# Fused attention and feed-forward on one core: the first pair's tokens kept in transposed order, an addition in unlike shapes, one query tile in another buffer, and a planner with new numbers

## The chip, the core and the metric

One core of a Trainium2 chip runs the whole program. The metric is the device time of one launch in microseconds. A core has a tensor engine (PE, for matmuls, with weight loads shown as PEld), VectorE (DVE), ScalarE (ACT), GpSimd (POOL) and SyncE (SP, whose queue issues every DMA of this kernel), all with instruction streams of their own that meet by semaphores.

## What is computed

Eight batches of eight heads with 576 tokens of 64 values each. A short set of 32 queries per head attends to the tokens, and then the tokens attend to those 32 results. The output of all heads, 512 values for each of 4608 tokens, goes through a feed-forward with GELU.

```python
def sm_attn(qq, kk, vv):
    s = scale * np.matmul(qq, kk.transpose(0, 1, 3, 2))
    s = s - np.max(s, axis=-1, keepdims=True)
    a = np.exp(s)
    a = a / (np.sum(a, axis=-1, keepdims=True) + 1e-09)
    return np.matmul(a, vv)
p_packed = sm_attn(p, k, v)
out = sm_attn(q, p_packed, p_packed)      # [8, 8, 576, 64]
x = out.transpose(0, 2, 1, 3).reshape(4608, 512)
h = x @ w_in                              # [512, 2048]
g = 0.5 * h * (1.0 + erf(h * inv_sqrt2))
return g @ w_out                          # [2048, 512]
```

## The kernel before

**Stages.** The batches are worked on in four pairs. For a pair, the attention gives two things: the packed result `pp` (32 values per head) and the weights `a2` of the second softmax. The product a2 x packed is never made: `packed_w_in` forms W' = packed x W_in for each batch, and the hidden layer is W' x a2. W_in and W_out are taken in four pieces of 512 hidden columns, so there are 16 units u = 4 x pair + piece. A unit has eight steps, four blocks c of 128 hidden columns for each batch j of the pair. In step n PE makes h (`hidden_steps`, L1117 for unit 0 and L1126 for the others), ACT applies GELU (`graw`, L1148) and rounds it to the high half of g (L1155), DVE makes the low half (L1157), and PE adds g x W_out into four PSUM tiles with three matmuls each (`three`, L1178 to L1180, twelve o matmuls per step). The 64 tokens per batch that fill no tile of 128 are cast on POOL (L1168, L1169) and multiplied as the edge tile (`o_edge`). `finish` copies or adds the sums to `acc` (L1259, L1264) and the last unit of a pair stores them (L1269). Unit 0 uses plain float32 for h, in 8 matmuls per step instead of 12 of the rounded type.

**Loads.** Keys and queries come as two tiles of 576 KB per batch (`load`), for the first pair as whole rows (L499), for later pairs as four DMAs with short rows (L509). The weights come as 64-bit words of 512 KB (L984, L988). In the first four units they are decoded by ACT (L994, L995), DVE (L1002 to L1008) and POOL (L1022 to L1036), stored as float32 (`keep`, L1041), and read back by later pairs (L962).

**The first pair's attention.** Keys and queries are transposed by PE (L537) and copied back (L541), the packed queries at L574. The first scores are at L602, the softmax at L669 to L695, the packed result at L744 to L762. The second scores come back transposed by DVE (L780). Then each group of 32 weights gets its maximum (L798) taken off (L823), the exponential (L829), its sum (L837), EPS added (L838), the reciprocal (L839) and the product (L842), the last transpose into `a2` (L848, in the first pair, where it also restores the order of tokens with a strided write; L854 in the others) and the split into two rounded halves (L856, L858). One of the four chunks of the first pair has L823 and L842 on POOL.

**What sets the order.** `Order` runs the whole program as a set of tasks in a model with a cost in us for each operation, once dry and once for good, and writes out the instructions of each engine in the order in which the model issued them. Priorities come from the chain of operations behind each one, with the tables `SLACK` and `EARLY` by kind of task. `LATER` and `FIRST` hold the steps of attention stages and of loads. A `Ring` is a set of buffers with a fixed order of users. In the result each engine, SP's queue too, executes strictly in its order and waits at the first instruction that isn't ready. Where the model has PE with nothing to do before the first output step, it writes a filler, a small matmul on zeros (`keep_warm`, L1099). In steady state an operation on PE that isn't of a step is taken as ready `MARGIN` = 2 us later than the model says.

Of the kernel before, what the change touches and what calls it, by code (L numbers as in the profile page):

```python
# [42 lines left out]
DMA_FIRST, DMA_ISSUE, DMA_START, DMA_END, DMA_RATE = 2.0, 0.5, 0.6, 0.9, 390e3  # L43

DMA_DEPTH = 8
TABLE_SWITCH = 1.3
PE_START, PE_WINDOW, PE_LEAST = 1.0, 3.41, {True: 0.45, False: 0.9}
# [4 lines left out]
    "batch0": 1.967,  # L52
    "batch1": 2.254,
    "attention": 2.432,
    "load0": 0.822,
    "load": 4.206,
    "w_in0": 3.279,
    "w_out0": 2.28,
    "w_in": 1.0,
    "w_out": 1.839,  # L60
    "packed_w_in": 1.201,
# [3 lines left out]
    "batch0": 0,  # L65
    "batch1": 2.3,
    "attention": 0,
    "load0": 0.7,
    "load": -23.7,
    "w_in0": -0.9,  # L70
    "w_out0": -0.6,
    "w_in": 0,
    "w_out": -10.3,
    "packed_w_in": -2.4,
    "steps": -3.6,
}

MARGIN = 2.0

# [14 lines left out]
    "weights2": (31.8, 53.8, 41.5, 53.2),  # L94
    "groups1": ((0, 1, 2, 3),),
# [23 lines left out]
    "copy": ("ACT", "ACT", "ACT", "ACT"),  # L119
    "banks": (True, False, False, True),  # L120
# [5 lines left out]
    "turn": {"k": ("DVE", "ACT", "ACT", "ACT"), "q": ("ACT", "DVE", "ACT", "ACT")},  # L126
# [80 lines left out]
def tails_of(done):  # L207

    tails, of = {}, [0.0] * len(done)
    for n in reversed(range(len(done))):  # L210
        key, time, by, kind = done[n]
        of[n] += time * SLACK[kind]
        tails[key] = of[n] + EARLY[kind]
        for x in by:
            of[x] = max(of[x], of[n])
    return tails
# [10 lines left out]
class Order:  # L227
# [4 lines left out]
    def __init__(self, tails=None):  # L232
# [7 lines left out]
        self.free[PE] = PE_START  # L240

# [24 lines left out]
    def advance(self, task, value, engine):  # L266
# [16 lines left out]
        if isinstance(what, Op):  # L283
# [11 lines left out]
            entry = (0 if self.dry else -self.tails[key], self.serial, what, lambda v, e: go_on(v, e, by), after)  # L295
# [34 lines left out]
    def issue(self, engine):  # L330
# [15 lines left out]
        if engine == DMA:  # L346
            n, size = op.cost
            end = self.now
            for _ in range(n):
                end = max(end, self.under_way[-DMA_DEPTH])  # L350
                self.link = max(self.link, end + DMA_ISSUE + DMA_START) + size / n / DMA_RATE
                end += DMA_ISSUE
                self.under_way.append(max(self.link, end + DMA_START) + DMA_END)
# [33 lines left out]
def packed_attention_gelu_ffn(ctx: ExitStack, tc: tile.TileContext, q, k, v, p, w_in, w_out, out):  # L387
# [27 lines left out]
    def plan(order):  # L415
# [6 lines left out]
        def small(b):  # L422

            return psum_o if b < 2 else wide
# [14 lines left out]
        mx2s = ring("mx2", 2, [P, 3, 4, NB32])  # L439
# [14 lines left out]

        wps[1].names = ["v_0_1"] + [f"wp_{u}_1" for u in range(NU)]
# [32 lines left out]
        class Chunk:  # L488
            def __init__(self, bt, hh):
                self.bt, self.b, self.hh, self.i, self.n = bt, bt.b, hh, 2 * bt.j + hh, f"{bt.b}_{hh}"  # L490
# [4 lines left out]

        def load(bt, name, src, c, step):

            def rows(t):
                nc.sync.dma_start(t, src[bt.b, 4 * c:4 * c + 4].rearrange("h (x s) d -> (h x) (s d)", s=2 * NT))  # L499
# [11 lines left out]
            cost, fn = ((1, 590e3), rows) if bt.b < 2 else ((4, 1475e3), blocks)  # L511
            bt.raw[name, c] = yield Op(DMA, cost, step, fn, [(xraws, f"{name}_{bt.n}_{c}")])
            fire(bt.loaded[name, c])

        def transposed(bt, name, c, step):
            yield bt.loaded[name, c]
            raw = bt.raw[name, c]
            if bt.b < 2:
# [3 lines left out]
                yield [turn(raw, t, i, engine, step, f"{name}m_{bt.n}_{c}_{i}", hold) for i in range(3)]  # L522
# [6 lines left out]
            xraws.give(raw)  # L529
# [22 lines left out]
        def load_values(s, step):  # L552
# [8 lines left out]
            s.v = yield Op(DMA, (2, 660e3), step, fn, [(s.v_ring, f"v_{s.n}")])  # L561
            fire(s.v_loaded)

        def packed_queries(bt, step):
# [11 lines left out]
            m = yield Op(PE, 0.22, step, product, [(small(bt.b), f"pTm_{bt.n}")])  # L576
# [5 lines left out]
            small(bt.b).give(m)  # L582
# [116 lines left out]
        def packed(s, step):  # L699

            e1T = yield Op(PE, 0, step, lambda t: None, [(e1ts, f"e1T_{s.n}")], busy=False, hold=held("packed", s))
            ring_ = small(s.b)
# [92 lines left out]
        def greatest2(s, step):  # L795
            yield Op(
                DVE, 0.67, step,
                lambda: nc.vector.tensor_reduce(s.mx2[:, 0, s.i], blocks(s.e2), axis=AX.X, op=ALU.max))  # L798
# [17 lines left out]
        def softmax2(ss, step):  # L816
            n, m = len(ss), ss[0].mx2

            def centre(s):
# [3 lines left out]
                    lambda: on(engine).tensor_tensor(u, u, per_block(m[:, 0, s.i]), ALU.subtract), port=True)  # L823
# [519 lines left out]
```

## Time and profile before

| | |
|---|---|
| median of 3 runs | 744.21 us (743.89 to 745.51) |
| span of the profiled execution, first to last instruction | 740.1 us |
| its own time | not on the page; the median lies 4.1 us above its span |
| PE busy | 726.6 us, 98% |
| DVE, ACT, POOL busy | 391.8, 350.8, 149.3 us |
| granted clock of PE | 0.999 |
| moved by DMA | 106.75 MB, 83.89 read from and 22.02 written to HBM |

A row of a group of instructions reads: line, engine, operation, out<-in by the program's names, shapes, count, then busy time and mean duration of one in ns, and after the second bar the idle time of the engine just before them, with what ended it. A row of a timeline reads: start, duration, engine, line, and in brackets the idle time ahead of it and who ended it. A row of a window reads: from:to, its length, then busy time (and instructions) of PE, PEld, DVE, ACT and POOL, the granted clock, the mean DMA share and GB/s. `SPq` is the issue of a DMA by SP, not its transfer. Records of PE overlap: an o matmul's record lasts 0.39 us, and the next one starts 0.23 us after it.

### The profile page before, as it was taken

Reading aid. Unit: us, or ns where it says so; the run is one execution under the profiler, and the core shown is the slowest. Engines: PE = TensorE matmul, PEld = TensorE weight load, DVE = VectorE, ACT = ScalarE, POOL = GpSimd, SP = SyncE. Lnnn points to the kernel's source line nnn. Section 1 sums busy time; section 2 is a strip of 40 time slices with the busy share of each in tenths; the row PEclk is TensorE's granted clock in tenths of the full one; section 3 lists DMA queues with packets and bytes.
Section 4 is the critical chain, followed back from the end, with each engine's and each line's share of the span. In section 5 each row is a group of like instructions: output and inputs, shape, how many; then the busy total and the mean of one; then the engine's idle time right before and its main releaser. Section 6 shows DMA issues by size and latency. Waiting matters only on the chain.

```text
span 740.1 us, 13183 instructions
## 1 busy us (share of the span) xinstructions
PE 726.6 (98%) x5292; PEld 583.6 (79%) x5292; DVE 391.8 (53%) x614; ACT 350.8 (47%) x597; POOL 149.3 (20%) x312
## 2 busy tenths in 40 slices
PE   8999999998999999999999999999999999999997
PEld 5778776886778788788777878788877888888886
DVE  4798748887775323723767331652558322333332
ACT  5866667765653343733455343463455344323321
POOL 1446453644310001010010101010011011101010
PEclk9999999999999999999999999999999999999999
DMA  9999984685417994252143996332141602112031
GB/s 298 356 152 305 208 245 165 206 236 195 171 59 211 182 171 153 33 171 65 46 184 95 206 174 233 40 118 88 33 171 58 243 1 99 74 47 96 1 114 71
DMA packets 156157, 106.75 MB, mean 144 GB/s; under 512 B 123841, under 2 KB 132033, under 8 KB 156097
## 3 DMA queue, kind: packets, MB, share of 16 engines
q1 hardware_dynamic: 156096, 105.93, 53.7%
q8 instruction: 41, 0.67, 0.4%
q14 instruction: 20, 0.16, 0.1%
HBM read 83.89 MB, written 22.02 MB: 143 GB/s over the span
## 4 chain that ended last, share of the span: by engine, by line
PE 78%; DMA 10%; DVE 4%; ACT 3%; SPq 2%; issue 2%; POOL 1%; DVEq 0%; ACTq 0%; POOLq 0%
PE h L1126 23%; PE o L1178 14%; PE o L1180 13%; PE o L1179 13%; DMA k<-in_k_dram 4%; PE wps L1060 3%; DMA wraw<-in_moe_w_out_dram 3%; PE s L602 2%; PE o_edge L1178 2%; DMA wraw<-in_moe_w_in_dram 2%; PE o_edge L1180 2%; PE o_edge L1179 2%; PE pp L744 1%; SPq L509 1%; DMA q<-in_q_dram 1%
## 5 line engine op out<-in xcount | busy, mean ns | idle before, releaser
L1126 PEld LDWEIGHTS h<-a2T,wp 128*128 128x128 f32 x1440 | 202.2, 188 | 17.1 <-ACT graw L1148 2.2
L1126 PE MATMUL h<-a2T,wp 128*128 128x288 f32 x1440 | 211.3, 296 | 2.4 <-ACT graw L1148 0.8
L1178 PE MATMUL o<-w,g 128*128 128x512 f32 x508 | 205.4, 404 | 0.3 <-ACT g L1155 0.3
L1180 PE MATMUL o<-w,g 128*128 128x512 f32 x508 | 199.5, 393 | 1.7 <-DVE g L1157 1.7
L1179 PE MATMUL o<-w,g 128*128 128x512 f32 x508 | 198.4, 391 | 0.0
L1148 ACT ACTIVATE graw<-h 128x576 f32<-128x576 f32 x128 | 83.3, 651 | 241.6 <-PE h L1126 223.2
L1157 DVE TENSOR_TENSOR g<-graw,g 128x512 fp32r<-128x512 f32 x128 | 92.8, 725 | 169.5 <-ACT g L1155 168.9
L1168 POOL CAST t<-graw 128x64 fp32r<-128x64 f32 x128 | 37.1, 290 | 492.3 <-ACT graw L1148 360.6
L1178 PEld LDWEIGHTS o<-w,g 128*128 128x128 f32 x508 | 95.5, 188 | 41.3 <-issue 21.3
L1180 PEld LDWEIGHTS o<-w,g 128*128 128x128 f32 x508 | 95.4, 188 | 26.4 <-DVE g L1157 5.2
L1179 PEld LDWEIGHTS o<-w,g 128*128 128x128 f32 x508 | 95.5, 188 | 14.4
L1264 DVE TENSOR_TENSOR acc<-o,acc 128x512 f32<-128x512 f32 x96 | 63.7, 684 | 40.5 <-PE o L1180 40.5
L1155 ACT CAST g<-graw 128x512 fp32r<-128x512 f32 x128 | 79.4, 621 | 9.3 <-PE o L1180 6.0
L1076 DVE TENSOR_TENSOR wp<-wps,wp 128x1024 fp32r<-128x1024 f32 x30 | 36.7, 1222 | 36.2 <-ACT wp L1071 36.2
L1071 ACT CAST wp<-wps 128x1024 fp32r<-128x1024 f32 x30 | 30.4, 1012 | 44.0 <-PE wps L1060 44.0
L1169 POOL TENSOR_TENSOR t<-graw,t 128x64 fp32r<-128x64 f32 x128 | 46.6, 364 | 10.2
L1060 PE MATMUL wps<-w,pp 64*32 64x512 f32 (+1 forms) x528 | 34.6, 581 | 0.6 <-DVE e L780 0.6
L994 ACT ACTIVATE wt<-wraw 128x512 f32<-128x512 f32 x32 | 21.6, 675 | 23.9 <-DMA wraw<-in_moe_w_out_dram 9.6
L526 DVE STREAM_TRANSPOSE kT<-k 128x1152 f32<-128x1152 f32 x12 | 16.5, 1376 | 26.9 <-DMA k<-in_k_dram 26.9
L1030 POOL TENSOR_TENSOR wt<-wt 128x512 int32<-128x512 int32 x16 | 20.7, 1296 | 39.4 <-DVE wt L1008 30.2
L1022 POOL TENSOR_TENSOR w<-wt 128x512 int32<-128x512 int32 x16 | 21.7, 1357 | 29.5 <-ACT kT L541 12.5
L1002 DVE TENSOR_SCALAR wt<-wt 128x512 f32<-128x512 f32 x32 | 16.5, 516 | 19.5 <-ACT wt L994 19.4
(115 smaller groups left out, 673.6 us busy)
## 6 DMA issues: line engine op xcount, KB each, us to landing
w<-ws SPq DMA_DIRECT2D x72, 512.0 KB, 4.9
ws<-w SPq DMA_DIRECT2D x24, 512.0 KB, 4.2
out_dram<-acc SPq DMA_DIRECT2D x36, 256.0 KB, 2.7
wraw<-in_moe_w_in_dram SPq DMA_DIRECT2D x16, 512.0 KB, 5.5
v<-in_v_dram SPq DMA_DIRECT2D x16, 512.0 KB, 6.1
wraw<-in_moe_w_out_dram SPq DMA_DIRECT2D x16, 512.0 KB, 4.8
k<-in_k_dram SPq DMA_DIRECT2D x48, 144.0 KB, 4.7
q<-in_q_dram SPq DMA_DIRECT2D x48, 144.0 KB, 4.6
```

The costliest lines, as they stand in the source:

```text
L1060: nc.tensor.matmul(t[r0:r0 + 32, hh, :m], lhsT=pp[b][rows, hh, r0:r0 + 32], rhs=wi[u, hh][rows, g, cols], start=True, stop=True)
L1076: yield Op(DVE, 1.2, step, lambda: nc.vector.tensor_tensor(lo, x, hi.bitcast(F32), ALU.subtract))
L1126: nc.tensor.matmul(t[:, half, :HALF], lhsT=w[:, wpart, ch, fc], rhs=a2T[b, ch][:, apart, half * HALF:(half + 1) * HALF], start=ch == 0 and ...
L1148: lambda raw: nc.scalar.activation(raw.rearrange("p (a n) -> p a n", a=2), t[:, :, :HALF], AF.Gelu),
L1155: g = yield Op(ACT, 0.52, lead, lambda g: nc.scalar.copy(g[:, 0], main), [(gts, f"g_{n}")])
L1157: DVE, 0.6, lead, lambda: nc.vector.tensor_tensor(g[:, 1], main, g[:, 0].bitcast(F32), ALU.subtract),
L1168: nc.gpsimd.tensor_copy(dst[:, 0], side)
L1169: nc.gpsimd.tensor_tensor(dst[:, 1], side, dst[:, 0].bitcast(F32), ALU.subtract)
L1178: nc.tensor.matmul(t, lhsT=g[0], rhs=w[:, 0], start=first, stop=False)
L1179: nc.tensor.matmul(t, lhsT=g[0], rhs=w[:, 1], start=False, stop=False)
L1180: nc.tensor.matmul(t, lhsT=g[1], rhs=w[:, 0], start=False, stop=last)
L1264: yield Op(DVE, 0.6, n, lambda: nc.vector.tensor_tensor(a, x, a, ALU.add))
```

## The change

**The first pair's tokens.** The last transpose of `weights2` writes contiguously and leaves the tokens in the order (n, x) instead of x * 18 + n. All that follows works on tokens alike, so the order stays until `finish` stores the rows of pair 0 with a strided view of the output. The middle tile holds tokens of both batches and takes two DMAs instead of one.

**EPS.** The buffer of the second softmax's sums gets three columns more, the sums are laid out as 3 groups of 6 with a pitch of 7, and the addition reads that and writes 18 in a row.

**A query tile.** `q_0_1`, the second query tile of batch 0, goes into the buffer that later holds the first W', as `v_0_1` did with the second.

**PSUM.** All second scores of the first pair take a wide tile (`banks` all False). 

**The planner.** DMA operations have new costs, and a short-row load counts as two of the DMAs under way. In steady state an operation that waits for a DMA is taken as ready `DMA_MARGIN` = 3 us later. A change between PE instructions on the whole array and in parts costs 0.1 us in the model. A later pair's attention starts when the given output step (`from`: the third, or the first) has its g. Single tasks get offsets of priority (`SOONER`), and `SLACK` and `EARLY` have new numbers.

```diff
-DMA_FIRST, DMA_ISSUE, DMA_START, DMA_END, DMA_RATE = 2.0, 0.5, 0.6, 0.9, 390e3
+DMA_FIRST, DMA_ISSUE, DMA_START, DMA_END, DMA_RATE = 2.5, 0.5, 0.6, 0.9, 390e3
+MODE_SWITCH = 0.1
 SLACK = {
-    "load": 4.206,
+    "load": 0.122,
...
 EARLY = {
-    "load": -23.7,
+    "load": 21.2,
...
+SOONER = {
+    "softmax2_0_1": -53.3,
...
+DMA_MARGIN = 3.0
...
+    "from": (2, 0, 2, 0),
...
-    "banks": (True, False, False, True),
+    "banks": (False, False, False, False),
+    "small": (True, True, True, True),
+    "together": True,
...
+            if engine == DMA and self.steady:
+                after += DMA_MARGIN
+            first = 0 if self.dry else -self.tails[key] - SOONER.get(key, 0) - (SOONER.get(what.takes[0][1], 0) if what.takes else 0)
...
+            if engine == PE and op.cost and op.busy != self.whole:
+                self.whole = op.busy
+                begin += MODE_SWITCH
...
-        mx2s = ring("mx2", 2, [P, 3, 4, NB32])
+        mx2s = ring("mx2", 2, [P, 3, 4, NB32 + 3])
...
+        wps[0].names = ["q_0_1"] + [f"wp_{u}_0" for u in range(NU)]
...
+        def raw_ring(bt, name, c):
+            return wps[0] if (bt.b, name, c) == (0, "q", 1) else xraws
...
-            cost, fn = ((1, 590e3), rows) if bt.b < 2 else ((4, 1475e3), blocks)
+            cost, fn = ((1, 590e3), rows) if bt.b < 2 else ((4, 1640e3, 2), blocks)
...
-            s.v = yield Op(DMA, (2, 660e3), step, fn, [(s.v_ring, f"v_{s.n}")])
+            s.v = yield Op(DMA, (2, 830e3), step, fn, [(s.v_ring, f"v_{s.n}")])
...
             def inverse():
-                nc.vector.tensor_reduce(z, u, axis=AX.X, op=ALU.add)
-                nc.vector.tensor_scalar(z, z, EPS, None, ALU.add)
-                nc.vector.reciprocal(r, z)
+                apart = z.rearrange("p (a b) -> p a b", a=3)[:, :, :NB32 // 3]
+                nc.vector.tensor_reduce(apart, u.rearrange("p (a b) n -> p a b n", a=3), axis=AX.X, op=ALU.add)
+                nc.vector.tensor_scalar(r, apart, EPS, None, ALU.add)
+                nc.vector.reciprocal(r, r)
...
-                yield Op(
-                    DVE, 1.3, step,
-                    lambda: nc.vector.transpose(raw.rearrange("p (x n) -> p n x", n=NB32), blocks(s.e2)))
+                yield Op(DVE, 0.69, step, lambda: nc.vector.transpose(raw, s.e2))
...
-                if n % STEPS == 0:
+                yield g_ready[n]
+                if n % STEPS == LATER["from"][n // STEPS]:
                     fire(pair_started[n // STEPS])
-                yield g_ready[n]
...
-                yield Op(DMA, (1, 262e3), n, lambda: nc.sync.dma_start(out[r0:r0 + P], a))
+                def fn():
+                    if pr:
+                        nc.sync.dma_start(out[r0:r0 + P], a)
+                        return
+                    for j in range(2):
+                        rows = out[j * S:(j + 1) * S].rearrange("(x n) d -> n x d", n=NB32)
+                        n0, n1 = max(4 * i - j * NB32, 0), min(4 * i + 4 - j * NB32, NB32)
+                        if n0 < n1:
+                            p0 = 32 * (n0 + j * NB32 - 4 * i)
+                            nc.sync.dma_start(rows[n0:n1], a[p0:p0 + 32 * (n1 - n0)])
+                yield Op(DMA, (1 if pr or i != 4 else 2, 262e3), n, fn)
```

More of the change, by code (lines that the diff above doesn't have):

```diff
@@ L521, in transposed @@
                 hold = FIRST["hold"][name][2 * bt.j + c]
-                yield [turn(raw, t, i, engine, step, f"{name}m_{bt.n}_{c}_{i}", hold) for i in range(3)]
+                yield [turn(raw_of(raw), t, i, engine, step, f"{name}m_{bt.n}_{c}_{i}", hold) for i in range(3)]
             else:
@@ L581, in packed_queries @@
                 [(pts, f"pT_{bt.n}")])
-            small(bt.b).give(m)
+            small(2 * bt.j, bt.b).give(m)
             fire(bt.p_ready)
@@ L873, in attention @@
             for bt in bts:
-                kind = "attention" if pr else f"batch{bt.j}"
-                loading = "load" if pr else "load0"
-                start(packed_queries(bt, plan["p"][bt.j]), kind)
+                start(packed_queries(bt, plan["p"][bt.j]), "attention" if pr else f"batch{bt.j}")
                 for c in range(2):
-                    start(load(bt, "k", k, c, plan["k"][2 * bt.j + c]), loading)
-                    start(load(bt, "q", q, c, plan["q"][2 * bt.j + c]), loading)
+                    for name, src in (("k", k), ("q", q)):
+                        start(load(bt, name, src, c, plan[name][2 * bt.j + c]), "load" if pr else "load0")
             for s in ss:
@@ L882, in attention, with kind_of @@
                 s.v_ring = wps[1] if (s.b, s.hh) == (0, 1) else vraws
-                start(load_values(s, plan["v"][s.i]), loading)
+                start(load_values(s, plan["v"][s.i]), "load" if pr else "load0")
+            def kind_of(s, which):
+                return f"attention {which}" if pr else f"batch{s.j} {which}_{s.n}"
             def group(members, softmax, step):
@@ L891, in task @@
                     fire(after)
-                start(task(), "attention" if pr else f"batch{members[0] // 2}")
+                start(task(), kind_of(ss[members[0]], softmax.__name__))
                 return {i: (before, after) for i in members}
@@ L965, in weight @@
                 return
-            yield [decode(u, i, part, *at) for part, at in enumerate(zip(load_steps, steps))]
+            kind = f"w_{'in' if i < 2 else 'out'}"
+            yield [
+                (decode(u, i, part, *at), kind if u else f"{kind}0 {n}_{part}")
+                for part, at in enumerate(zip(load_steps, steps))]
             d = scratch[f, i] = None if order.dry else dram.tile([P, 2, FB], F32, name=f"ws_{f}_{i}")
@@ L1280, in later_pair @@
             yield scored[pr - 1]
-            plan = {key: x if "groups" in key else [(pr - 1) * STEPS + y for y in x] for key, x in LATER.items()}
+            plan = {key: x if key in ("from", "groups1", "groups2") else [(pr - 1) * STEPS + y for y in x] for key, x in LATER.items()}
             yield from attention(pr, plan)
```

105 lines of the change are left out of this document (69 added, 36 removed).

## The prediction

> **What bounds the kernel now.** I read the page first, then busy time by stretches, then the tensor engine's timeline for each stretch in which it loses time, and last the queue behind that loss.
>
> ```profile
> span 740.1 us, 13183 instructions
> PE 726.6 (98%) x5292; PEld 583.6 (79%) x5292; DVE 391.8 (53%) x614; ACT 350.8 (47%) x597; POOL 149.3 (20%) x312
> 0.00:57.00 57.00, 53.76 (x664) 39.62 (x665) 41.43 (x84) 40.00 (x81) 20.01 (x25) 1.00 1.00 267
> 100.00:120.00 20.00, 18.69 (x148) 13.86 (x147) 14.12 (x24) 13.51 (x26) 12.24 (x17) 1.00 0.72 254
> 170.00:176.00 6.00, 4.35 (x21) 3.23 (x20) 4.07 (x5) 3.80 (x8) 2.10 (x2) 1.00 0.43 171
> 244.00:258.00 14.00, 13.01 (x79) 9.55 (x78) 6.87 (x7) 5.60 (x9) 1.11 (x4) 1.00 1.18 197
> 418.00:433.00 15.00, 14.26 (x86) 10.69 (x85) 7.08 (x7) 5.84 (x10) 1.41 (x5) 1.00 1.30 196
> 57.00:736.00 679.00, 672.56 (x4631) 544.00 (x4628) 349.67 (x530) 310.85 (x517) 129.26 (x288) 1.00 0.51 134
> L1099 PE MATMUL idle<-still 128*128 128x256 bf16 x180 | 25.2, 285 | 1.1 <-DVE still L411 1.1
> L1126 PE MATMUL h<-a2T,wp 128*128 128x288 f32 x1440 | 211.3, 296 | 2.4 <-ACT graw L1148 0.8 <-ACT e L662 0.7 <-ACT e1T L719 0.2
> ```
>
> PE is the bound: it idles 740.1 - 726.6 = 13.5 us. Of these 3.2 lie before the first output step at 57 us, 6.4 between 57 and 736, and the remaining 3.9 in the tail, which the change leaves. From 57 us on, four stretches hold 1.31 + 1.65 + 0.99 + 0.74 = 4.7 of the 6.4. And 25.2 us of the busy time is no work: the 180 filler matmuls, which the planner puts where it expects PE to have nothing.
>
> So the time is real matmuls + fillers + unplanned waits + tail. The order of the changed program holds the same real matmuls, form by form, so an edit can act only on fillers, waits and the cost of going from one kind of matmul to another.
>
> **Fillers.** The changed order has 201 instead of 180, and they begin early: 49 before the first key transpose instead of 18.
>
> ```profile
> 1.05 2.74 PE L1099 MATMUL idle<-still 128*128 128x256 bf16 x12 [1.05 <-DVE still L411]
> 5.94 0.55 PE L537 MATMUL idle<-ident,k 128*128 128x128 f32 x3 [0.46 <-DMA k<-in_k_dram]
> 7.50 1.17 PE L537 MATMUL km<-ident,k 128*128 128x128 f32 x9 [0.35 <-DMA k<-in_k_dram]
> 40.76 0.67 PE L1060 MATMUL wps<-w,pp 64*32 64x256 f32 x16 [0.58 <-DVE e L780]
> 41.36 5.96 PE L1099 MATMUL idle<-still 128*128 128x256 bf16 x53
> 47.28 2.18 PE L1117 MATMUL h<-a,wp 128*128 128x288 f32 x8
> ```
>
> The 53 fillers from 41.36 to 47.28 take 0.11 us each; the first twelve some 0.22. The added ones stand behind the first 3 us, so 21 x 0.11 = **+2.3 us** (4.6 at most, at 0.22). PE executes them whether it has to wait or not. The late start comes from SP: two 512 KB pieces of W_in now lead the keys.
>
> SP's queue from its first row, before:
> ```order
> L568 DMA p_85<-in_p_dram 128x2x64 x2
> L499 DMA k_0_90<-in_k_dram 128x1152
> L499 DMA k_1_94<-in_k_dram 128x1152
> L499 DMA k_0_98<-in_k_dram 128x1152
> L988 DMA wraw_0_0_102<-in_moe_w_in_dram 128x2x512
> ```
> and now:
> ```order
> L623 DMA p_84<-in_p_dram 128x2x64 x2
> L1046 DMA wraw_0_0_89<-in_moe_w_in_dram 128x2x512
> L1046 DMA wraw_0_1_93<-in_moe_w_in_dram 128x2x512
> L553 DMA k_0_97<-in_k_dram 128x1152
> L553 DMA k_1_101<-in_k_dram 128x1152
> ```
> The keys moved behind 1 MB. PE's first key row starts at 5.94 and the one with the next 576 KB at 7.50, so 1 MB is worth some 2.8 us.
>
> **Waits in the start.** Without the 1.05 before the first matmul the 57 us hold 2.2 us of unplanned idle, the three rows above with a wait 1.4 of it. The new costs plan loads later, so part of it is now paid as fillers. Two edits shorten VectorE's chain there besides.
>
> ```profile
> 34.13 1.28 POOL L1030 TENSOR_TENSOR wt<-wt 128x512 int32<-128x512 int32 x1 [2.80 <-DVE wt L1008]
> 35.89 1.16 POOL L842 TENSOR_TENSOR e<-e,mx 128x576 f32<-128x576 f32 x1 [0.48 <-ACT qT L541]
> 34.66 0.78 DVE L838 TENSOR_SCALAR mx<-mx 128x18 f32<-128x18 f32 x1
> 36.39 0.69 DVE L838 TENSOR_SCALAR mx<-mx 128x18 f32<-128x18 f32 x1
> L838 DVE TENSOR_SCALAR mx<-mx 128x18 f32<-128x18 f32 x4 | 2.6, 640 | 0.1
> L838 DVE TENSOR_SCALAR mx<-mx 128x18 f32<-128x18 f32 x16 | 4.9, 305 | 0.5
> L848 DVE STREAM_TRANSPOSE a<-e 128x576 f32<-128x576 f32 x4 | 4.7, 1244 | 0.0
> L854 DVE STREAM_TRANSPOSE a<-e 128x576 f32<-128x576 f32 x12 | 9.3, 772 | 0.1
> ```
>
> The EPS additions at L838 end when POOL's instruction ends (35.44 against 35.41, 37.08 against 37.05): they wait for POOL. The other twelve take (4.9 - 2.6)/12 = 0.19, so the unlike shapes can save 4 x 0.45 = 1.8 us of VectorE at most, and nothing at least. The Trainium skill, "SBUF — State Buffer", section "SBUF: two separate sides", has VectorE and GpSimd share a port pair, locked for a whole instruction; "VectorE: DVE Perf Modes", section "What auto-detection actually checks", gives the two-port mode to a single-source op whose outermost dimensions are both even or equal. Eighteen against eighteen qualifies, three against eighteen does not. By the rule the two additions at 34.66 and 36.39, which stand ahead of the first h, give back 0.78 + 0.69 - 2 x 0.19 = 1.1 us and the sum below would be 740.5; if the shapes change nothing it is 741.6; I count half. The transposes of the first pair lose their strided write: 4 x (1.244 - 0.772) = 1.9 us, half of it on the way to the first h; the planner has that already and it is net in the fillers. Of the 2.2 us of waits I take **-1.3** (ends 0 and -2.2), more than half because keys and VectorE both improve.
>
> **100 to 120 us and 170 to 176.** Up to 110 us the next unit's weights come late: on SP the W_in words of unit 1 stand behind twelve small-row key DMAs of pair 1, its W_out words behind sixteen. Now W_in and half of W_out stand ahead of all of these. The idle is 1.31, and each restart hides 0.16 more (a record of 0.39 against a pace of 0.23), with three restarts 1.8: **-1.4** (ends 0 and -1.8), since the chain may find its next limit soon. The clearest loss follows:
>
> ```profile
> 172.02 0.40 PE L1180 MATMUL o<-w,g 128*128 128x512 f32 x1
> 174.07 0.33 PE L758 MATMUL ppTm<-ident,pn 128*128 128x128 f32 x1 [1.65 <-DVE wp L1076]
> 170.62 0.66 ACT L994 ACTIVATE wt<-wraw 128x512 f32<-128x512 f32 x1 [2.30 <-DMA wraw<-in_moe_w_out_dram]
> 171.76 0.99 ACT L1071 CAST wp<-wps 128x1024 fp32r<-128x1024 f32 x1
> ```
>
> ACT sits 2.3 us at the decoding of a late W_out piece; wp, g and the pp copies, for which PE and VectorE wait, queue behind it. PE loses 174.07 - 172.02 - 0.23 = 1.8 us. ACT's order there, before:
> ```order
> L1148 ACTIVATE graw_2153<-h_2131 128x576
> L994 ACTIVATE wt_3_0_2165<-wraw_3_0_2113 128x512
> L995 ACTIVATE wt_3_0_2165<-wraw_3_0_2113 128x512
> L1071 CAST wp_0_1982<-wps_0_0_2156 128x1024
> L1155 CAST g_2183<-graw_2153 128x512
> L1027 CAST w_2_2189<-wt_2_0_2115 128x512
> L762 COPY pp_2198<-ppTm_0_2191 128x128
> ```
> and now:
> ```order
> L1213 CAST g_2199<-graw_2180 128x512
> L1129 CAST wp_0_1971<-wps_0_0_2183 128x1024
> L817 COPY pp_2214<-ppTm_0_2197 128x128
> L1085 CAST w_2_2223<-wt_2_0_2192 128x512
> L817 COPY pp_2214<-ppTm_1_2232 128x128
> L1052 ACTIVATE wt_3_0_2250<-wraw_3_0_2149 128x512
> ```
> The decoding stands behind all of them: **-1.8** (0 if another load takes its place).
>
> **Key loads of pairs 2 and 3.**
>
> ```profile
> 231.09 0.39 PE L1178 MATMUL o_edge<-w,t 128*128 128x512 f32 x1
> 235.94 5.85 SPq L509 DMA_DIRECT2D k<-in_k_dram  x4
> 239.27 0.69 DVE L1157 TENSOR_TENSOR g<-graw,g 128x512 fp32r<-128x512 f32 x1 [1.98 <-ACT g L1155]
> 245.21 1.38 DVE L526 STREAM_TRANSPOSE kT<-k 128x1152 f32<-128x1152 f32 x1 [5.24 <-DMA k<-in_k_dram]
> 246.51 0.65 DVE L1157 TENSOR_TENSOR g<-graw,g 128x512 fp32r<-128x512 f32 x1
> ```
>
> VectorE waits for a key tile, and the g that PE needs stands behind it. Idle 0.99 + 0.74 plus six restarts of 0.16 is 2.7 us. VectorE's order for pair 2 from its first key transpose, before (one g per step):
> ```order
> L526 STREAM_TRANSPOSE kT_0_2848<-k_0_2785 128x1152
> L1157 TENSOR_TENSOR g_2856<-graw_2850,g_2856 128x512
> L1157 TENSOR_TENSOR g_2893<-graw_2888,g_2893 128x512
> L526 STREAM_TRANSPOSE kT_1_2932<-k_1_2826 128x1152
> L1157 TENSOR_TENSOR g_2934<-graw_2926,g_2934 128x512
> ```
> and now:
> ```order
> L1215 TENSOR_TENSOR g_2870<-graw_2864,g_2870 128x512
> L1215 TENSOR_TENSOR g_2908<-graw_2898,g_2908 128x512
> L581 STREAM_TRANSPOSE kT_0_2933<-k_0_2837 128x1152
> L1215 TENSOR_TENSOR g_2949<-graw_2943,g_2949 128x512
> L581 STREAM_TRANSPOSE kT_1_2974<-k_1_2900 128x1152
> ```
> The second tile stands behind one g more, and so do those after it, in pair 3 behind two. A step is 12 o of 0.23 and 12 h (211.3 us / 120 = 1.76), 4.5 us. But SP issues the loads later too. I take **-2.0** (ends 0 and -2.7).
>
> **Changes of kind.** A block in 32-row form costs PE twice:
>
> ```profile
> 81.30 0.39 PE L1180 MATMUL o<-w,g 128*128 128x512 f32 x1
> 81.61 1.09 PE L1060 MATMUL wps<-w,pp 64*32 64x512 f32 x16
> 82.63 0.50 PE L1178 MATMUL o<-w,g 128*128 128x512 f32 x1
> 82.97 0.39 PE L1179 MATMUL o<-w,g 128*128 128x512 f32 x1
> ```
>
> 0.31 to enter instead of 0.23, and 0.34 for the first o behind it. The new order enters or leaves such blocks 102 times instead of 96: 6 x 0.1 = **+0.6**. The Trainium skill, "TensorEngine Tiling (Array Packing)", "Key Properties", says that a change of tiling mode drains the engine; this rule speaks against the change, and the trace agrees at 0.1 us a side.
>
> **At nothing.** The query tile in the W' buffer moves one 576 KB load, covered by the loads around it; without that cover it costs its place in the queue, counted under the second rival. PSUM for the first scores and the later start of a pair show in fillers. The stores of pair 0 stay rows of 2 KB; the tenth DMA costs SP some 0.4 us, behind 4 us steps.
>
> New waits of a new order: bounded by 0 and by the 1.7 us outside the four stretches, doubled; I take **+0.4**.
>
> Sum: 2.3 + 0.6 - 1.3 - 1.4 - 1.8 - 2.0 + 0.4 = -3.2. The execution's span of 740.1 becomes 736.9; around it lie 744.2 - 740.1 = 4.1 us against the median shown, so 741.0 us.
>
> **Rivals.**
> 1. Everything helps: all waits named and the 2.2 us go, none come: 744.2 + 2.9 - 2.2 - 1.8 - 1.8 - 2.7 = 738.6, and 736.9 if the other 1.7 go too. For it: all have one cause, something queued behind a load. Against: the start is bound by loads whose bytes are unchanged.
> 2. The keys stay late. On SP they now stand behind a W_out reload that needs a buffer freed by the edge products (231.09). Four issues of 5.85 end at 254.5, and the last tile is there 245.21 - 241.79 = 3.4 later, 257.9. Its g is due four steps after 239.27, its transpose 1.4 earlier, at 255.9. That is 2.0 us late: 743.0, no change. Against: issue gets quicker when less is under way.
> 3. Slower: on SP the last query tile of the first pair now stands behind four stores of decoded weights, which wait for POOL. Before it landed at 32.6, and the last transpose of its attention weights ended at 58.0, 25.4 us later.
>
> ```profile
> 25.10 7.48 DMA q<-in_q_dram
> 54.00 1.03 SPq L1041 DMA_DIRECT2D ws<-w  x1
> 55.67 2.34 DVE L848 STREAM_TRANSPOSE a<-e 128x576 f32<-128x576 f32 x2
> ```
>
>    By pace the first o now comes at 57.0 + 2.3 - 1.3 less two h of 2.0 and two W' products of 0.6 (the rows at 47.28 and 40.76 without the overlap of the last record), which move behind it: 52.8. Three o of 2.8, two h and two W' products later, at 66.4, the fifth h needs that tile. A landing up to 41 costs nothing, one after 45.7 eats the gain and 1.5 us more. By bytes it lands at 42 (seven transfers of 512 KB more, 1.4 us each); before, the store of the second W_out piece, which now stands ahead of it, left only at 54.0. At 48, halfway, 7 us are lost: 748. Against: that piece is loaded nine rows earlier on SP, and much of the 25.4 us is waiting behind the other batch.
> 4. The refit does nothing but add fillers: 744.2 + 2.9 = 747.1.
>
> **Chances.** Forecast 0.45 (739.5 to 742.6 by itself), rival 1 0.20, rival 2 0.20, rival 3 0.10, rival 4 0.05. A measurement of this kernel can tell 0.2%, 1.5 us. Faster is the first two and a little of the third: 0.68; same 0.18; slower 0.14. The range from 737.0 to 745.0 leaves out part of rival 1 and the slower ones.
>
> **What would show it.** Right: some 28 us of fillers, first o near 53 us, no PE gap over 0.5 us near 172, and VectorE's waits for k under 2 us each. Wrong on EPS: L838's successor still above 0.4 us in the first pair. Wrong altogether: h of batch 1 waiting for a2 behind q, or PE idle between 57 and 736 above 5 us.

## The result and the profile after

The changed kernel takes 749.67 us in the median (746.70 to 751.50, 6 runs), the kernel before beside it 744.29 (742.42 to 746.38, 6 runs). The ratio estimated from these runs is 1.0064 with a 95% interval of 1.0040 to 1.0088 (the quotient of the two medians is 1.0072): slower by 0.6%, where 741.0 us and a gain were forecast. The measurement lies above the range of 737.0 to 745.0.

Of the changed kernel: two lines of the page, the stretches that the prediction spoke of, and the group of fillers.

```profile
span 747.7 us, 13236 instructions
PE 729.9 (98%) x5313; PEld 588.6 (79%) x5313; DVE 392.7 (53%) x614; ACT 355.9 (48%) x601; POOL 149.7 (20%) x312
0.00:57.00 57.00, 53.56 (x645) 40.36 (x646) 40.02 (x80) 40.12 (x79) 22.22 (x24) 1.00 0.88 305
100.00:120.00 20.00, 20.00 (x142) 15.72 (x142) 12.35 (x19) 11.15 (x20) 8.96 (x15) 1.00 1.06 238
170.00:176.00 6.00, 6.00 (x43) 4.25 (x43) 3.14 (x5) 4.03 (x7) 1.41 (x3) 1.00 0.57 190
230.00:265.00 35.00, 25.23 (x122) 21.14 (x121) 6.81 (x9) 8.60 (x14) 2.80 (x10) 0.90 0.69 140
418.00:433.00 15.00, 15.00 (x85) 13.31 (x84) 3.46 (x4) 5.58 (x10) 2.25 (x8) 1.00 1.16 233
57.00:736.00 679.00, 668.50 (x4636) 542.09 (x4636) 348.59 (x529) 314.77 (x522) 126.92 (x286) 0.99 0.51 130
L1157 PE MATMUL idle<-still 128*128 128x256 bf16 x201 | 27.2, 287 | 1.1 <-DVE still L455 1.1
```

PE is busy 3.3 us more and idle 17.8 us instead of 13.5. Three of the four stretches are clean: no idle is left in 100 to 120 us, in 170 to 176, and at the keys of pair 3 (418 to 433). Between 57 and 736 us PE idles 679.00 - 668.50 = 10.5 us; more than 5 there was the prediction's own sign of being wrong altogether. Nearly all of it lies in one stretch, 35.00 - 25.23 = 9.8 us between 230 and 265. The same stretch of the kernel before:

```profile
230.00:265.00 35.00, 34.01 (x193) 28.09 (x192) 12.49 (x14) 12.56 (x20) 4.47 (x16) 1.00 1.10 194
```

Both are the start of unit 4, where the keys of pair 2 arrive. PE's rows with a wait there, changed kernel:

```profile
242.83 0.47 PE L1236 MATMUL o<-w,g 128*128 128x512 f32 x1 [1.65 <-DMA w<-ws]
251.61 0.80 PE L1238 MATMUL o<-w,g 128*128 128x512 f32 x1 [3.73 <-DVE g L1215]
262.10 0.79 PE L1238 MATMUL o<-w,g 128*128 128x512 f32 x1 [4.39 <-DVE g L1215]
```

PE waits 3.73 and 4.39 us for g and 1.65 us for a W_out piece, 9.8 us together. The two long waits cost it a second time. Behind the first of them come

```profile
252.20 0.63 PE L1236 MATMUL o<-w,g 128*128 128x512 f32 x1
252.62 0.63 PE L1237 MATMUL o<-w,g 128*128 128x512 f32 x1
```

Five or six o matmuls behind each start 0.43 us apart instead of 0.23 and last 0.63 us instead of 0.39, before the usual pace is back; the granted clock of the stretch is 0.90. VectorE shows why g is late:

```profile
249.60 1.38 DVE L581 STREAM_TRANSPOSE kT<-k 128x1152 f32<-128x1152 f32 x1 [10.62 <-DMA k<-in_k_dram]
250.90 0.65 DVE L1215 TENSOR_TENSOR g<-graw,g 128x512 fp32r<-128x512 f32 x1
260.09 1.38 DVE L581 STREAM_TRANSPOSE kT<-k 128x1152 f32<-128x1152 f32 x1 [8.54 <-DMA k<-in_k_dram]
264.49 1.38 DVE L581 STREAM_TRANSPOSE kT<-k 128x1152 f32<-128x1152 f32 x1 [2.45 <-DMA k<-in_k_dram]
```

It is the picture that the prediction showed for the kernel before (5.24 us for a key tile, g queued behind it), at twice the size. SP's queue in the same place:

```profile
223.72 1.19 SPq L1017 DMA_DIRECT2D w<-ws  x2
225.30 4.28 SPq L1337 DMA_DIRECT2D out_dram<-acc  x4
229.67 4.14 SPq L1017 DMA_DIRECT2D w<-ws  x3
233.87 12.94 SPq L563 DMA_DIRECT2D k<-in_k_dram  x4
246.91 1.12 SPq L1337 DMA_DIRECT2D out_dram<-acc  x2
248.07 14.77 SPq L563 DMA_DIRECT2D k<-in_k_dram  x10
```

The four DMAs of the first key tile occupy SP for 12.94 us; before, the four that the prediction showed, of the second tile, took 5.85. Ahead of them are four stores of pair 0 and three W_out reloads. What the stores do is read from the share of the DMA engines while they run (the last two numbers of a window's row: mean share of 16 engines, GB/s). The changed kernel:

```profile
229.00:231.50 2.50, 2.50 (x13) 2.07 (x12) 1.22 (x2) 0.60 (x1) 0.56 (x2) 1.00 0.25 84
```

and the kernel before, at its stores:

```profile
234.50:235.50 1.00, 1.00 (x6) 0.83 (x5) 0.15 (x1) 0.97 (x2) 0.41 (x2) 1.00 1.02 376
```

A share of 0.25 is 4 engines of 16, where before all 16 were at work, and 84 GB/s instead of 376. Both move rows of 2 KB, which take about as long each. Counted from the packet records of the two traces:

```
                           2 KB packets per us   ns of one packet   engines at work on them
before, 234.5 to 235.5 us          181                 87                15.7
changed, 231 to 238 us              49                 85                 4.2
```

A strided store has the shape 4 x 32 rows. It is carried by as many engines as its outermost dimension counts, and its 128 rows take 32 x 84 ns = 2.7 us on these four instead of 8 x 84 ns = 0.7 us on sixteen. Four such stores hold them for 10.8 us, and a key tile is not there until they are through. The packet records show this too: of the 1152 packets of 128 bytes of the first key DMA, 864, which is twelve sixteenths, ran between 237.3 and 239.2 us, and no key packet followed until 242.5 us; the stores ran until 241.1 us, and packets of a W_out reload behind them. The Trainium skill states this rule: "DMA: Bandwidth & Descriptors", section "Why a DMA increments its semaphore by 16 and not by 1", has a DMA use the largest number of engines up to 16 that divides the slowest dimension of both its access patterns, the lowest-numbered ones; its "Rules for kernel authors" advise a multiple of 16 outermost. The trace agrees with 4.2 engines for a dimension of 4. The prediction did not weigh that rule.

### The profile page after: what moved, and what is told of

It reads as the page before. It is cut to its first block, busy times and chain, and to the rows that moved or that the text cites. A ratio compares the mean times of both kernels' runs of the same rounds, so it can differ in the third digit from the quotient of the medians.

```text
span 747.7 us, 13236 instructions
## 1 busy us (share of the span) xinstructions
PE 729.9 (98%) x5313; PEld 588.6 (79%) x5313; DVE 392.7 (53%) x614; ACT 355.9 (48%) x601; POOL 149.7 (20%) x312
## 4 chain that ended last, share of the span: by engine, by line
PE 87%; SPq 3%; DMA 3%; DVE 3%; ACT 2%; issue 1%; POOL 1%; ACTq 0%; DVEq 0%; POOLq 0%
PE h L1184 24%; PE o L1236 16%; PE o L1238 15%; PE o L1237 15%; PE wps L1118 4%; SPq L563 3%; PE o_edge L1236 2%; PE o_edge L1238 2%; PE o_edge L1237 2%; PE h L1175 2%; PE s L657 2%; DMA k<-in_k_dram 2%; DMA wraw<-in_moe_w_out_dram 1%; PE pp L799 1%; PE e1Tm L761 1%
## 5 line engine op out<-in xcount | busy, mean ns | idle before, releaser
L1215 DVE TENSOR_TENSOR g<-graw,g 128x512 fp32r<-128x512 f32 x128 | 95.4, 746 | 195.4 <-ACT g L1213 195.2
L1226 POOL CAST t<-graw 128x64 fp32r<-128x64 f32 x128 | 35.2, 275 | 513.6 <-ACT graw L1206 393.1
L1157 PE MATMUL idle<-still 128*128 128x256 bf16 x201 | 27.2, 287 | 1.1 <-DVE still L455 1.1
```

Of the source, the lines that this page charges most:

```text
L1215: DVE, 0.6, lead, lambda: nc.vector.tensor_tensor(g[:, 1], main, g[:, 0].bitcast(F32), ALU.subtract),
L1226: nc.gpsimd.tensor_copy(dst[:, 0], side)
```

## The experiments

Three causes were open at first: the cut of the stores (A), the order on SP, with the keys behind a W_out reload (B, the prediction's second rival), and the start (C).

**Stores in one piece.** In the changed kernel:

```diff
-                    if pr:
+                    if pr or i != 4:
                         nc.sync.dma_start(out[r0:r0 + P], a)
```

> The changed kernel, but pair 0's tiles (all but the one that lies in both batches) are stored as 128 rows in one piece, so its tokens stay in the transposed order in the output; nothing else moves. Theory A (a strided store, 4 x 32 rows, is carried by 4 of the 16 DMA engines: 48 packets of 2 KB per us at 84 ns each = 4.0 engines busy, 185 per us before; the keys of pair 2 queue behind it): PE's two long waits at 247 and 257 us go, about 9.8 us of idle and 1.5 of restarts, 749.7 becomes about 738.5 (737 to 741). Theory B (the keys are late because SP issues them behind a W_out reload, the second rival of the prediction): stays at 749 to 750, both waits stay above 3 us. Theory C (the whole start is slower through the fillers and the late first keys): 747 or more.

740.51 us, ratio to before 0.9947 (0.9929 to 0.9965): this is what theory A says, and B and C fall. One long wait of PE is left in the stretch, behind the one tile that was still cut, into two stores of 2 x 32 rows:

```profile
254.63 0.80 PE L1238 MATMUL o<-w,g 128*128 128x512 f32 x1 [5.41 <-DVE g L1215]
```

**Stores by n.** The order of tokens stays right:

```diff
-                            nc.sync.dma_start(rows[n0:n1], a[p0:p0 + 32 * (n1 - n0)])
+                            for n in range(n0, n1):
+                                p0 = 32 * (n + j * NB32 - 4 * i)
+                                nc.sync.dma_start(rows[n], a[p0:p0 + 32])
```

> The changed kernel with the right order of tokens, but each strided store of 4 x 32 rows is made as four DMAs of 32 rows. Theory A: with 32 rows outermost a store spreads over 16 engines again; 27 DMAs more at 0.4 us of SP's time each, where SP has slack, so 738.5 to 740. Theory B: 749 to 750. A third theory, D (rows 36 KB apart in HBM are slow to write, however they are cut): 748 to 750, with the 2 KB packets as slow as in the changed kernel.

738.91 us, ratio 0.9926 (0.9905 to 0.9948). D falls too: the rows lie in HBM as far apart as in the changed kernel. The stretch and its two waits, of which the expectations further on count only the first:

```profile
230.00:265.00 35.00, 31.61 (x183) 26.35 (x182) 11.49 (x13) 11.96 (x19) 4.35 (x14) 1.00 1.03 192
246.63 0.50 PE L1238 MATMUL o<-w,g 128*128 128x512 f32 x1 [1.29 <-DVE g L1215]
253.37 0.50 PE L1238 MATMUL o<-w,g 128*128 128x512 f32 x1 [2.10 <-DVE g L1215]
```

Behind these shorter waits the o matmuls keep their usual 0.23 us.

**The old order with strided stores.** The same cut, put into the kernel before (`fn` as in the changed kernel's diff):

```diff
-                yield Op(DMA, (1, 262e3), n, lambda: nc.sync.dma_start(out[r0:r0 + P], a))
+                yield Op(DMA, (1, 262e3), n, fn)
```

> The kernel before, with pair 0's stores cut as in the changed kernel (4 x 32 rows each; the output's tokens are then in the wrong order), nothing else moved. Theory A: each of the three stores between the key loads at 231.7 us holds 4 engines for 32 x 84 ns = 2.7 us, 8 us in all, and the keys behind them land later by about that: the three waits of VectorE for k grow by 4 to 8 us in sum, so 748 to 752. Theory B: 744, no change, since the order on SP is the old one.

758.17 us, ratio 1.0182 (1.0143 to 1.0221). The direction is theory A's; the size, 14 us, is about twice the 4 to 8 that I had worked out. I had counted only the three stores ahead of the second key tile, but a W_out reload, for which PE itself waits, lies behind them as well:

```profile
249.61 0.77 PE L1178 MATMUL o<-w,g 128*128 128x512 f32 x1 [5.21 <-DMA w<-ws]
254.48 1.38 DVE L526 STREAM_TRANSPOSE kT<-k 128x1152 f32<-128x1152 f32 x1 [13.56 <-DMA k<-in_k_dram]
```

**Two rows outermost.** If the outermost dimension sets the number of engines, 2 must be worse than 4:

```diff
-                            nc.sync.dma_start(rows[n0:n1], a[p0:p0 + 32 * (n1 - n0)])
+                            for n in range(n0, n1, 2):
+                                p0 = 32 * (n + j * NB32 - 4 * i)
+                                nc.sync.dma_start(rows[n:n + 2], a[p0:p0 + 64])
```

> The changed kernel, with each of pair 0's stores cut into two DMAs of 2 x 32 rows instead of one of 4 x 32. If the outermost dimension (2) sets how many DMA engines carry a store and the split begins at the same engine each time, the 2 KB packets run at 24 per us on 2 engines, each tile takes 64 x 84 ns = 5.4 us instead of 2.7, four tiles ahead of pair 2's keys 21.5 instead of 10.8: 758 to 772 us. If the engines rotate from one DMA to the next, 4 work as in the changed kernel: 749 to 751. If the number of DMAs is what costs, between these two.

761.14 us, ratio 1.0223 (1.0185 to 1.0261). A share of 0.13 is two engines; in the packet records 225 packets in 9 us at 84 ns are 2.1. The window, and PE's waits for a W_out reload and a g:

```profile
231.00:240.00 9.00, 9.00 (x54) 7.95 (x52) 1.39 (x2) 2.55 (x4) 1.13 (x4) 1.00 0.13 51
253.30 0.77 PE L1236 MATMUL o<-w,g 128*128 128x512 f32 x1 [13.25 <-DMA w<-ws]
272.58 0.80 PE L1238 MATMUL o<-w,g 128*128 128x512 f32 x1 [5.86 <-DVE g L1215]
```

Of the 1152 packets of the first key DMA 1008, fourteen sixteenths, ran between 248.4 and 250.4 us, and none until 253.3. A tile's two DMAs do not run side by side on four engines, so both take the same two. The Trainium skill says as much with the lowest-numbered engines ("DMA: Bandwidth & Descriptors", "Why a DMA increments its semaphore by 16 and not by 1").

**Another queue.** The strided stores, issued by ScalarE:

```diff
-                            nc.sync.dma_start(rows[n0:n1], ...)
+                            nc.scalar.dma_start(rows[n0:n1], ...)
```

> The changed kernel, its strided stores of 4 x 32 rows left as they are, but issued by ScalarE's queue instead of SP's (ten issues more in ScalarE's order near steps 32 to 36). The four DMA engines still spend 32 x 84 ns = 2.7 us on each. If pair 2's keys were late because they stand behind the stores in the same queue, another queue lets them pass: the waits for k fall below 2 us and the time is 738 to 741. If it is the four engines' time that lacks, whichever queue the packets come from, the four stores' 10.8 us stay in the way of the keys' share on these engines: 744 to 750.

747.57 us, ratio 1.0063 (1.0042 to 1.0083), where the changed kernel has 1.0064. Nothing comes back, and VectorE still waits 11.74 us for the first key tile, so it is the engines' time that lacks, not the place in the queue. The window, and the waits of VectorE and PE:

```profile
240.00:244.00 4.00, 4.00 (x25) 3.55 (x24) 0.69 (x1) 2.54 (x4) 1.12 (x4) 1.00 0.27 98
253.80 1.38 DVE L581 STREAM_TRANSPOSE kT<-k 128x1152 f32<-128x1152 f32 x1 [11.74 <-DMA k<-in_k_dram]
255.81 0.79 PE L1238 MATMUL o<-w,g 128*128 128x512 f32 x1 [8.94 <-DVE g L1215]
```

**EPS, in both plans.** First the new kernel with stores by n and the old form of the addition, then the kernel before with the new form alone:

```diff
-                nc.vector.tensor_scalar(r, apart, EPS, None, ALU.add)
+                nc.vector.tensor_scalar(z[:, :NB32], z[:, :NB32], EPS, None, ALU.add)
...
-                nc.vector.tensor_scalar(z, z, EPS, None, ALU.add)
+                nc.vector.tensor_scalar(r, apart, EPS, None, ALU.add)
```

> As the kernel with stores by n, but EPS is added in like shapes (18 to 18) as before, on the same plan. If the addition in like shapes waits for GpSimd (0.69 to 0.78 us in the first pair before, 0.17 now), the first pair's additions take some 0.7 us again and the time is up to 1.1 us above that of the kernel with stores by n; if the next instruction of VectorE then waits instead, the time is the same within 0.3 us.

> The kernel before with EPS added in unlike shapes and nothing else, on the same plan. If the wait for GpSimd belongs to the form of the addition, its four long ones (0.78, 0.69, 0.69, 0.40 us) become 0.17; the forecast counted half of 1.1 us as gained: 743.3. If the lock only moves to VectorE's next instruction, the four are short and the time is that of before within 0.3 us.

739.10 us (ratio 0.9937, 0.9910 to 0.9964) with the old form against 738.91 with the new: the same. In the new plan GpSimd does not run beside these additions of the first pair, and they take 0.17 to 0.18 us in either form, so this pair of runs does not show what the form is worth where GpSimd runs. Before with the new form: 744.82 against 744.71 (1.0011, 0.9990 to 1.0031). Its additions are short, with GpSimd running beside them as it did; VectorE's next instruction beside GpSimd, L1002, takes 0.64 us instead of 0.36:

```profile
34.88 0.17 DVE L839 TENSOR_SCALAR mx<-mx 128x18 f32<-128x18 f32 x1
35.99 0.17 DVE L839 TENSOR_SCALAR mx<-mx 128x18 f32<-128x18 f32 x1
36.38 0.64 DVE L1002 TENSOR_SCALAR wt<-wt 128x512 f32<-128x512 f32 x1
```

The form is what made them wait, as the rule has it that the prediction quoted from the Trainium skill ("VectorE: DVE Perf Modes", "What auto-detection actually checks"): 0.17 us against 0.78 and 0.69. The time shows no gain, but its interval reaches from -0.7 to +2.3 us, so the 0.55 us of the forecast are not ruled out in the plan of before.

**The order of tokens alone**, in the kernel before, stored by n:

```diff
-                    lambda: nc.vector.transpose(raw.rearrange("p (x n) -> p n x", n=NB32), blocks(s.e2)))
+                    lambda: nc.vector.transpose(raw, s.e2))
```

> The kernel before with the first pair's tokens in transposed order, stored by n (32 rows a DMA), on the same plan. The four transposes fall from 1.24 to 0.77 us; half of the 1.9 us was taken to lie on the way to the first h: first h 0.5 to 1.0 us earlier and 743 us if the stores cost nothing; SP issues 36 stores instead of 9 at 0.45 us each, which can hold pair 2's keys some 3 us longer: then 744 to 746.

747.90 us, ratio 1.0035 (1.0017 to 1.0053), above both forecasts. The four transposes take 0.75 us, but the first h is not earlier (48.37 against 47.28 us), and the 36 stores cost: PE idles 3.6 us between 230 and 265 us, where before has 1.0, and waits 2.36 us for a g behind one key tile:

```profile
252.44 0.50 PE L1180 MATMUL o<-w,g 128*128 128x512 f32 x1 [2.36 <-DVE g L1157]
```

What the order is worth without its stores is left to old_order below.

**Keys first.** On the kernel with stores by n, a priority of 60 us for `k_0_0`, `k_0_1` and `k_1_0` in `SOONER`, then the plan refitted, which moves other tasks too:

```diff
-SOONER = {
+SOONER = {"k_0_0": 60.0, "k_0_1": 60.0, "k_1_0": 60.0,
```

> The kernel with stores by n, in which the first three key loads get 60 us of priority, so that they lead SP's queue as before; the plan is refitted and has 191 fillers, 19 of them ahead of the first key transpose (201 and 49). If fillers and late keys are a loss, as the forecast had it, the ten cost 1.1 us and the time is 737 to 738. If the start is bound by the bytes to load and decode, whatever comes first, it stays at 738.5 to 740.

749.77 us, ratio 1.0073 (1.0048 to 1.0098): outside both branches, and no answer to its question. The refit put the last second scores of the first pair behind four output steps, and PE waited 3.45 us for the attention weights that come of them, 1.98 us before that for a piece of W_in that GpSimd decodes. The two rows are not the whole of the loss, and the rest was not followed:

```profile
72.52 1.95 PE L1118 MATMUL wps<-w,pp 64*32 64x512 f32 x12 [1.98 <-POOL w L1080]
79.79 6.53 PE L1175 MATMUL h<-a,wp 128*128 128x288 f32 x20 [3.45 <-DVE a L902]
```

**The planner told of four DMAs a store**, and **no margin for loads**, both on the kernel with stores by n:

```diff
-                yield Op(DMA, (1 if pr or i != 4 else 2, 262e3), n, fn)
+                yield Op(DMA, (1 if pr else 4, 262e3), n, fn)
...
-DMA_MARGIN = 3.0
+DMA_MARGIN = 0.0
```

> The kernel with stores by n, and the planner told that such a store is four DMAs instead of one or two: pair 2's key transposes then stand one step of VectorE later (after 36, 37, 38, 39 of the g products instead of 35, 36, 37, 38), 201 fillers as before. In the kernel with stores by n PE still waits 1.29 us at 246.6 us for a g behind a key; if that goes, 737.0 to 738.0; if later loads take its place, 738.5 to 739.5.

> The kernel with stores by n, DMA_MARGIN at 0 in the refitted plan (same 201 fillers, same places of the key transposes of pairs 2 and 3, 108 crossings into or out of 32-row blocks instead of 102). If the margin is what took away the waits of 100 to 120 us and of 172 us, these come back: plus 2 to 4 us, 741 to 743. If the new costs of the loads did it, only the six crossings are added, 0.6 us: 739 to 740.

748.13 us (1.0060, 1.0042 to 1.0078): both waits of the stretch are gone, but this refit has new ones elsewhere, 4.72 us at 185.5 and 2.66 at 289.2, not followed further. 741.31 us (0.9979, 0.9963 to 0.9994) without the margin. The time lies where I had put returning waits, but the trace does not show them: PE idles 0.5 us at the end of 100 to 120, behind a softmax instruction of ACT, and not at all near 172, so the margin was not what removed the waits for loads. Its profiled span is 1.2 us longer, and the matmuls, taken at the usual pace of each pair of kinds, about 1 to 2 us longer, with six more crossings into or out of 32-row blocks; what makes up the rest of its loss against the kernel with stores by n stays open. The longer new wait in the plan with four DMAs a store:

```profile
185.50 1.21 PE L657 MATMUL s<-qT,pp 64*32 64x288 f32 x16 [4.72 <-DVE e L848]
```

**Half of the fillers**, same plan:

```diff
+                    filled.append(t)
+                    if len(filled) % 2:
-                    nc.tensor.matmul(bank(t)[:, :256], lhsT=still[:, :P], rhs=still, start=True, stop=True)
+                        nc.tensor.matmul(bank(t)[:, :256], lhsT=still[:, :P], rhs=still, start=True, stop=True)
```

> The kernel with stores by n and the same plan, but every second filler is left out: 101 instead of 201. The forecast counted each added filler as 0.11 us of time, since PE executes it whether it has to wait or not: 100 fewer are 11 us of PE's work. If fillers only stand where PE would wait for loads and VectorE anyway, the time stays at 738 to 740 and PE's idle before 57 us grows by about 10 us; if they delay the work behind them, 730 to 735; if PE loses its clock without them, 741 or more and the granted clock or the pace of the first real matmuls falls.

738.45 us, ratio 0.9940 (0.9921 to 0.9958), against 738.91 and 0.9926: no difference that the intervals show. The start with half of the fillers:

```profile
0.00:57.00 57.00, 47.73 (x551) 33.53 (x552) 41.47 (x83) 41.29 (x81) 23.16 (x26) 0.94 0.87 305
```

and with all of them, the kernel with stores by n:

```profile
0.00:57.00 57.00, 53.11 (x648) 40.45 (x649) 39.82 (x80) 40.73 (x80) 22.18 (x24) 1.00 0.87 305
```

PE works 5.4 us less in the first 57 us and waits that much more. The granted clock falls to 0.94 in this stretch and costs nothing that shows in the time.

**The old order in the new plan.** The changed kernel with the strided transpose back, and every tile stored whole:

```diff
-                yield Op(DVE, 0.69, step, lambda: nc.vector.transpose(raw, s.e2))
+                yield Op(DVE, 0.69, step, lambda: nc.vector.transpose(raw.rearrange("p (x n) -> p n x", n=NB32), blocks(s.e2)))
...
-                    if pr:
+                    if True:
                         nc.sync.dma_start(out[r0:r0 + P], a)
```

> The changed kernel with one part undone and the plan as it is: the first pair's last transposes write with a stride again (four of 1.24 instead of 0.77 us), so the tokens are back in order and all nine tiles of pair 0 are stored as 128 rows in one DMA. If the transposed order is worth what the forecast took (half of 1.9 us on the way to the first h), this costs 0.9 us in the start; whole stores on all 16 engines take away the 11 to 12 us that pair 2's keys cost, and the remaining wait of 1.3 us that the kernel with stores by n still has: 737 to 738.5. If the order of tokens matters more than that for the start (the four transposes stand in the way of all that follows), 740 to 742. If something else than the stores makes the keys late, 748 or more.

736.35 us, ratio 0.9904 (0.9887 to 0.9922): the lowest of all, 1% under the kernel before, though its interval overlaps with that of stores by n. The order of tokens brings nothing that shows: the first o comes at 54.92 us, and in the traces of the changed kernel and of the five runs that share its plan and its order of tokens at 53.8 to 55.1. PE is idle for no moment of the stretch that cost the changed kernel 9.8 us, though the keys still stand behind the W_out reloads on SP:

```profile
230.00:265.00 35.00, 35.00 (x206) 30.10 (x205) 11.97 (x14) 13.02 (x21) 3.92 (x14) 1.00 1.16 209
240.69 1.38 DVE L581 STREAM_TRANSPOSE kT<-k 128x1152 f32<-128x1152 f32 x1 [1.94 <-DMA k<-in_k_dram]
245.88 1.38 DVE L581 STREAM_TRANSPOSE kT<-k 128x1152 f32<-128x1152 f32 x1 [2.80 <-DMA k<-in_k_dram]
250.88 1.38 DVE L581 STREAM_TRANSPOSE kT<-k 128x1152 f32<-128x1152 f32 x1 [3.02 <-DMA k<-in_k_dram]
255.62 1.38 DVE L581 STREAM_TRANSPOSE kT<-k 128x1152 f32<-128x1152 f32 x1 [2.79 <-DMA k<-in_k_dram]
```

VectorE's waits for a key are 1.9 to 3.0 us and end in time for g.

## Why the prediction was wrong, point by point

To set the terms against the traces I took PE's matmuls from start to start and called lost what exceeds the usual pace of that pair of kinds; fillers stand apart. The stretches are by each trace's own time, so work that moved across a border blurs them a little. The rows of 100 us and later that name a stretch hold within some 0.5 us however the usual pace is taken; those of fillers, kinds and 0 to 100 us shift by 1 to 3 us among each other.

| Term | forecast | before | changed | measured |
|---|---|---|---|---|
| fillers | +2.3 | 23.8 | 27.0 | +3.2 |
| waits, 0 to 100 us | -1.3 | 9.9 | 8.7 | -1.2 |
| 100 to 140 us | -1.4 | 5.3 | 3.3 | -2.0 |
| 165 to 185 us (the W_out decoding) | -1.8 | 3.6 | 1.7 | -1.9 |
| keys of pair 2, 230 to 270 us | half of -2.0 | 2.6 | 14.2 | **+11.6** |
| keys of pair 3, 400 to 440 us | half of -2.0 | 2.4 | 1.3 | -1.1 |
| kinds (all matmuls at the usual pace) | +0.6 | 657.6 | 658.4 | +0.8 |
| waits in all other stretches | +0.4 | 30.8 | 28.8 | -2.0 |

The last row holds 140 to 165, 185 to 230, 270 to 400 and all from 440 on. The measured column sums to +7.4; the span grew by 747.7 - 740.1 = 7.6, the medians by 5.4. Of the +11.6, 9.8 - 1.0 = 8.8 are more idle, and the rest is the slower pace behind the long waits.

**The step that failed** stands under "At nothing": "The stores of pair 0 stay rows of 2 KB; the tenth DMA costs SP some 0.4 us". The size of a row was taken for the cost of a store. What changed is how many engines share the rows, 4 instead of 16, and no cover was named for that. In its place the trace shows 11.6 us lost by PE where the keys behind them arrive: the same plan with stores that spread takes 738.9 (by n) or 736.35 (whole, old order), and the old plan with the new cut loses 14 us. Without this step the sum would still not have been exact: these two kernels gain 5 to 7 us on the kernel before, where -3.2 was the sum.

**The other named terms** came out within a microsecond each, for fillers and kinds only as far as the pace can be told; the waits in all other stretches, forecast at +0.4, came out at -2.0. That the moved decoding and the moved key transposes pay is borne out by stretches without idle; pair 3, whose stores ahead are whole, got just the -1.1 that pair 2 should have had.

**The fillers** were priced about right and understood wrongly. I counted them as work that delays what follows. Half as many leave the time as it is, so those left out stood where PE would have waited. The first key row came 3.6 us later, where the prediction had 2.8, and the first o is earlier by 1.9 us (57.00 before), not by 4.2:

```profile
9.53 0.55 PE L592 MATMUL idle<-ident,k 128*128 128x128 f32 x3 [0.48 <-DMA k<-in_k_dram]
55.10 0.50 PE L1236 MATMUL idle<-w,g 128*128 128x512 f32 x1
```

**EPS**: in the changed kernel the additions take 0.17 us each, but not because of their form, for eps_like has 0.18 in the old form. GpSimd starts only after them, and VectorE meets it at another instruction, L1061, which ends soon after GpSimd's does:

```profile
38.31 0.17 DVE L894 TENSOR_SCALAR mx<-mx 128x18 f32<-128x18 f32 x1
39.10 1.27 DVE L1061 TENSOR_SCALAR wt<-wt 128x512 int32<-128x512 int32 x1
38.93 1.16 POOL L898 TENSOR_TENSOR e<-e,mx 128x576 f32<-128x576 f32 x1 [2.95 <-ACT e L884]
```

L1061 takes 0.43 us when nothing holds it. In eps_like, with the old form, it is held just as long:

```profile
37.76 1.27 DVE L1061 TENSOR_SCALAR wt<-wt 128x512 int32<-128x512 int32 x1
```

So the 0.55 us that the sum counted as gained by the form are not there in the new plan: the refit, not the edit, took the additions out of GpSimd's way, and put another instruction in it.

**Rival 2** named the right place, the keys of pair 2, and a wrong cause. Its W_out reload stands in the same order in old_order, where no PE time is lost; its price was 2.0 us. **Rival 3** did not come: from 49 to 80 us no matmul of the changed kernel has a wait that its timeline shows, and its 748 lies near the measured time by chance. Its mechanism, h waiting for late attention weights, showed in keys_first, from another cause. **Rival 1** and **rival 4** (747.1) fall with the table: 4 comes near the measured time, but by adding fillers and no gains, while the trace has both gains and one large loss.

**Around the span** the forecast added 4.1 us, the distance of the profiled span from a median of other executions. In the six runs of the changed kernel the time is 1.7 to 1.8 us above the span of the same execution. The rest was a difference between executions; with 1.75 the forecast's 736.9 would have been 738.65 for an execution like the profiled one. As a forecast of the median, 744.2 - 3.2 = 741.0 stands.

## What to carry to other kernels

When a store or load is cut anew, count the engines, not the row size: the outermost dimension of its pattern, 4 or 2 or 128, decided here between some 0.7 and 5.4 us for the same 256 KB (8 or 64 packets of 84 ns one after the other), and the loads queued behind paid for it. A DMA that nobody waits for is not free: ask what stands behind it on the same engines. And after a refit, undo each edit on the new plan by itself: the version with the lowest time here keeps the new plan and drops the first of its edits.

## What the runs showed of the hardware that I had not expected

- A transfer on few engines slows transfers on the same engines from another queue too. With the stores on ScalarE's queue, 44 store packets (2 KB, 84 ns) and 43 key packets (128 bytes, 13 ns) ran per us on the four engines between 240 and 244 us: they alternate by count, at 98 GB/s in all. The Trainium skill, "DMA: Bandwidth & Descriptors", "Queues, rings and completion order", lets each engine go round the queues packet by packet; the equal counts agree.
- The issue of a load on SP can itself last long: in the changed kernel that of one key DMA lasted 7.7 us (234.49 to 242.19) and the next 3.9, against 0.6 us for the first of the four. Most of it fell into the time in which four engines were busy with stores (until 241.1 us); that SP waits until the engines take up its packets is my reading, and no run tests it alone.
- A store of 32 rows takes SP 0.45 us to issue, so 36 of them run at 69 packets per us, well under the 181 of whole stores; the key tiles behind them still come in time but for two waits of PE, 1.29 and 2.10 us.
